# One load of w_phi, a split first tile, and later GpSimd readiness behind transfers in an attention and mixer kernel

## The chip, the cores and the metric

The kernel runs on one core of a Trainium2 chip. The metric is the time of one execution on the device in microseconds. Three runs of the kernel before took 1091.71, 1095.12 and 1089.41 us; the median is 1091.71.

## What is computed

The reference is a linear attention followed by a token and channel mixer, in float32. Shapes: 8 batches, 8 heads, 576 tokens, head dimension 64, 128 features, 512 channels, 256 hidden tokens, 1536 hidden channels.

```
phi(x)  = p = x @ w_phi;  p -= max|p| over features;  concat(exp(p), exp(-p))
kv      = phi(k)^T @ v              z = sum of phi(k) over tokens
x       = (phi(q) @ kv) / (phi(q) @ z + 1e-6)        # heads side by side: 512 channels
u       = x + w_tok2^T-side of relu(x^T @ w_tok1)    # mixes the 576 tokens
out     = u + relu(u @ w_ch1) @ w_ch2                # mixes the 512 channels
```

w_phi is 64x128. The mixer's weights come as float64.

## The kernel before

The work is recorded by five generators, and then ordered. `keys` and `queries` walk over 32 units; a unit is one batch and a pair of heads. Of the first eight units (PLAIN = 8) the tiles of q and k come together from `in_qkp`, q on partitions 0 to 63 and k on 64 to 127 (`load_plain`, L669: two tiles of 128x512 and 128x640, named `pair`). Later units come as `raw` and are split into a high and a low part on the partitions (`stack`, L609: a ScalarE cast and a GpSimd subtraction, into `stk` and `stq`).

`less_max` (L621) multiplies a tile with w_phi (`ppk`, `ppq`, `ppt` in PSUM, for keys, queries and the tail of a query), takes the largest absolute value (`mxk`, `mxq`, `mxt`) and subtracts it (`pmk`, `pmq`, `pmt`). In the first eight units this reads `wp`, a tile of 128x2x128. Its half 1 has w_phi on partitions 64 to 127 and zeros above, for the keys; its half 0 has w_phi on partitions 0 to 63 and zeros below, for the queries. Before the change w_phi is loaded twice, by two transfers on ScalarE's queue (L525 and L526), the keys' half first; GpSimd writes the zeros. Later two VectorE instructions for each half make `wp2` from it, which the later units use.

`turn` transposes pmq into `pt`, exponentiates it into `qf` and `qh`, and takes the low part `ql`, on VectorE for one sign and on GpSimd for the other. `numerators` (L854) multiplies with `kv` into `pn` and copies pn to `u0` and `u1`. The row of denominators then goes through a round of transfers on SP's queue: `few` (two small ones), a reciprocal, `inv` to DRAM, and two broadcasts of `inv` into parts of u0 and u1. At L883 GpSimd multiplies u0 and u1 into `xt`. Four such xt (two head pairs, two parts of the tokens) are the input of one half mix, `token_mix` (L897), which transposes xt into `px` on TensorE, and goes through `xh` and `xl`, `pa`, `ah` and `al` to `ph`; there are 16 such half mixes, two for a batch. The channel stream (`uh`, `ul`, `h`, `gh`, `gl`, `acc`) works on 18 blocks of 256 tokens and fills TensorE between the pieces of the others.

`weave` (L1039) interleaves the generators, and `arrange` (L276) makes one order from what was recorded: a greedy pass over a model of the five engines and one bus, with a planned start and end for each operation. An operation that waits for another gets a ready time from the end of that other and a lag (L470). On GpSimd and VectorE the next operation is the one with the earliest ready time, shifted by its stream. The end of a transfer is planned as its issue cost (560 ns for the broadcasts), its bytes at 210 per ns on the one bus, and 1400 ns, or 1000 for small ones (L43, L432). The instructions are then emitted sorted by planned start, so each engine works them off in that order. Since the pass is greedy, another ready time early on can change the order of everything behind it. The operations on `wp2` are emitted at 20 us of planned time.

Of the kernel before, what the change touches and what calls it, by code (L numbers as in the profile page):

```python
# [18 lines left out]
B, H, S, D = 8, 8, 576, 64  # L19
# [27 lines left out]
HOLD = 120.0  # L47
SLACK, EASE, CALM = 200, 1000, 8.0e5
PATIENCE = 0
LATER = 2.0e4  # L50
BEAT = 10240 / 3

# [202 lines left out]
def urge(op, t):  # L255
    if op.stream == "" or op.unit == "tensor":
        return op.pri
    return t + HEAD[op.stream]


def choose(ready, u, t, held):
    import heapq
    if u in ("vector", "gpsimd"):
        other = held["gpsimd" if u == "vector" else "vector"]
        if other > t + HOLD + PATIENCE:
            late = []
            while ready and (u == "gpsimd" or ready[0][2].shut):
                late.append(heapq.heappop(ready))
            got = heapq.heappop(ready) if ready else heapq.heappop(late)
            for x in late:  # L270
                heapq.heappush(ready, x)
            return got[2]
    return heapq.heappop(ready)[2]


def arrange(ops):  # L276
# [84 lines left out]
    def slots(r):  # L361
        if r.tag not in free:
            free[r.tag] = [0.0] * r.bufs
        return free[r.tag]

    def offer(op):
        r = op.first
        if r is not None:
            key = (r.tag, r.line)
            if turn[key] != r.place or not slots(r):  # L370
                waiting.setdefault(r.tag, []).append(op)
                return
            t = max(op.ready, min(slots(r)) + (LOAD if op.unit == "tensor" else 0.0))
        else:
            t = op.ready
        heapq.heappush(soon[op.unit], (t, op.pri, op.seq, op))
# [4 lines left out]
    def beat(end):  # L381
        while (beats[0] + 1) * BEAT <= end:
            share = spent.pop(beats[0], 0.0) / BEAT
            beats[0] += 1
            if slow[0]:
                slow[0] = share < 0.76
            else:
                slow[0] = share < 0.375

    def spend(t, end, work):  # L390
        k = int(t // BEAT)
        while k * BEAT < end:
            part = min(end, (k + 1) * BEAT) - max(t, k * BEAT)
            spent[k] = spent.get(k, 0.0) + work * part / (end - t)
            k += 1
    order, count = [], 0
    while count < len(ops):
        best = None
        for u in units:
            s, q = soon[u], ready[u]  # L400
            while s and s[0][0] <= clock[u]:
                t, pri, seq, op = heapq.heappop(s)
                heapq.heappush(q, (urge(op, t), seq, op))
            t = clock[u] if q else (s[0][0] if s else None)
            if t is not None and (best is None or t < best[0]):
                best = (t, u)
        if best is None:
            raise RuntimeError("nothing can be placed")
        t, u = best
        if ready[u]:  # L410
            op = choose(ready[u], u, t, held)
        else:
            op = heapq.heappop(soon[u])[3]
        r = op.first
        if r is not None:
            key = (r.tag, r.line)
            if turn[key] != r.place or not slots(r):
                waiting.setdefault(r.tag, []).append(op)
                continue
            have = slots(r)  # L420
            k = min(range(len(have)), key=lambda k: have[k])
            t = max(t, have.pop(k))
            turn[key] += 1
            again = waiting.pop(r.tag, [])
            for x in again:
                offer(x)
        op.start = t
        if op.name == "dma_start":
            t = max(t, BEGIN)
            clock[u] = t + op.cost  # L430
            bus[0] = max(t + op.cost, bus[0]) + op.bytes / RATE
            op.end = bus[0] + LANDING[0 if op.small else 1]  # L432
        elif u == "tensor":
            beat(t)
            pace = 2.0 if slow[0] else 1.0
            c = max(op.cost * pace if op.args[2].root.dtype != F32R or op.name == "transpose" else
                    max(op.cost, (op.cost - 4) * pace), LOAD * pace)
            rows = (op.args[1].lo, op.args[1].hi, op.args[0].lo, op.args[0].hi)
            if op.name == "transpose" or rows[1] - rows[0] == rows[3] - rows[2] == P:
                t = max([t, *(end + TURN for end in tiles.values())])  # L440
                tiles.clear()
                clock[u] = t + c
            else:
                t = max(t + (0 if tiles else TURN), tiles.get(rows, 0.0))
                tiles[rows] = t + c
                clock[u] = t + 14
            op.end = t + c + FILL
            spend(t, t + c, op.work * pace)
        else:
            op.end = t + op.cost  # L450
            if op.shut or u == "gpsimd":
                other = held["gpsimd" if u == "vector" else "vector"]
                op.end = max(op.end, other + op.cost - HOLD)
                held[u] = op.end
            clock[u] = op.end
        order.append(op)
        count += 1
        for r in op.roots:
            r.left -= 1
            r.done = max(r.done, op.end)  # L460
            if r.left == 0:
                slots(r).append(r.done + 40)
                for x in waiting.pop(r.tag, []):
                    offer(x)
        for x, soft in op.before:
            lag = 0.0 if x.unit == op.unit and u != "gpsimd" else LATE[x.unit]
            if soft or x.unit == op.unit == "tensor":
                got = op.start
            else:
                got = op.end + lag + (LOAD + (SLACK if op.end < CALM else EASE) if x.unit == "tensor" else 0.0)  # L470
            x.ready = max(x.ready, got)
            x.need -= 1
            if x.need == 0:
                offer(x)
    for op in order:
        if op.roots and op.roots[0].kw.get("name") == "wp2":
            op.start = LATER
    order.sort(key=lambda op: op.start)
# [4 lines left out]
def mixer_kernel(ctx, tc, qk, qkp, vals, w_phi, w1, w1t, w2, wc1, wc2d, out):  # L483
    real, nc = tc.nc, Recorder()
# [37 lines left out]
    make_identity(real, ident.made())  # L522
    wp2 = st.tile([P, 2, F], F32R, tag="wp2", name="wp2", bufs=1)
    wp = cst.tile([P, 2, F], F32, name="wp")
    for j in (1, 0):  # L525
        nc.scalar.dma_start(wp[j * D:j * D + D, j], w_phi)  # L526
    for j in (1, 0):
        nc.gpsimd.memset(wp[j * D:j * D + D, 1 - j], 0.0)
    ones = cst.tile([P, D], F32, name="ones")
# [139 lines left out]
    def load_plain(i):  # L669

        out = []
        for k, (c, n) in enumerate(((0, 512), (512, 640))):
            t = wk.tile([P, n], F32, tag=f"{'kq'[i % 2]}{k}", name=f"pair{i}{k}", bufs=1)
            nc.sync.dma_start(t, qkp[i, :, c:c + n])
            out.append(t)
        pairs[i] = out

    def keys():
# [3 lines left out]
        for i in range(B * NP):  # L682
            yield from until(lambda: i < 2 or i - 2 in asked)
            if i < PLAIN:
                load_plain(i)
            else:
                load(i)
# [378 lines left out]
    def never(mixed):  # L1066
        return False

    weave([(keys(), 5.2, bool), (queries(), 5.2, bool), (token_stream(), 8.0, lambda mixed: not mixed),
           (load_weights(), 10.0, never), (channel_stream(), 19.5, never)])  # L1070
    order = arrange(nc.ops)
    with tc.manual_schedule():
        for op in order:
# [52 lines left out]
```

## Time and profile before

| | |
|---|---|
| median of three runs | 1091.71 us |
| the profiled execution's own time | 1091.3 us |
| its span, first to last instruction | 1089.5 us |
| TensorE matmul busy | 1071.7 us, 98% |
| VectorE | 652.7 us, 60% |
| ScalarE | 585.3 us, 54% |
| GpSimd | 527.3 us, 48% |
| DMA | 65.24 MB, mean 60 GB/s |

In the profile PE is TensorE's matmul, PEld its weight load, DVE VectorE, ACT ScalarE, POOL GpSimd, SP the engine that issues most transfers; a q behind a name is the engine's queue of issues. Times of rows count from the span's start. A row names an instruction by what it writes and reads, out<-in; nearly all instructions have the line L175, a recorder's, so the tile names tell them apart. Idle time before an instruction stands in brackets, with what ended it.

### The profile page before, as it was taken

The page shows a single profiled execution, that of the slowest core. Times are in us where ns is not written, and L with a number is a line of the kernel's source. Part 1 is how long each engine was busy: PE and PEld are TensorE (multiplying, and loading weights), DVE is VectorE, ACT ScalarE, POOL GpSimd, SP SyncE. Part 2 cuts the span into 40 slices and gives each one's busy share as a digit, 9 for nine tenths or more (in the row PEclk, how much of TensorE's full clock was granted, in tenths as well). Part 3 has the DMA queues.
Part 4 walks back from the last instruction along what each step waited for, and adds up shares of the span by engine and source line. Part 5 has one row for each costly group of instructions (what it writes and reads, how often), then busy time and mean ns, then how long its engine had stood idle before and what let it go on. Part 6 is the DMA issues. An engine that isn't in the chain of part 4 may idle for free.

```text
span 1089.5 us, 23678 instructions
## 1 busy us (share of the span) xinstructions
PE 1071.7 (98%) x8880; PEld 1022.5 (94%) x8880; DVE 652.7 (60%) x1442; ACT 585.3 (54%) x1613; POOL 527.3 (48%) x660
## 2 busy tenths in 40 slices
PE   8999999999999999999999999999999999999998
PEld 7988997999999899999999999999999999999998
DVE  6898975566667667676666676676666543211111
ACT  5777654566656566566566566566666543211110
POOL 1244443566756565666556566575665633101110
PEclk9999999999999999999999999999999999999999
DMA  6565522111121211112121212112121101000000
GB/s 190 164 187 157 177 63 59 46 48 46 47 66 47 59 48 45 47 50 57 34 66 46 66 44 63 47 24 66 47 61 33 42 13 38 1 20 20 21 20 20
DMA packets 61090, 65.24 MB, mean 60 GB/s; under 512 B 28272, under 2 KB 47856, under 8 KB 60976
## 3 DMA queue, kind: packets, MB, share of 16 engines
q1 hardware_dynamic: 60672, 63.33, 21.0%
q8 instruction: 70, 1.15, 0.4%
q10 hardware_dynamic: 304, 0.40, 0.1%
q14 instruction: 44, 0.36, 0.1%
HBM read 53.97 MB, written 9.58 MB: 58 GB/s over the span
## 4 chain that ended last, share of the span: by engine, by line
PE 91%; DMA 3%; DVE 2%; issue 1%; POOL 1%; ACT 1%; SPq 0%; ACTq 0%; DVEq 0%; POOLq 0%
PE h L175 26%; PE acc L175 26%; PE pn L175 9%; PE pkv L175 8%; PE pa L175 5%; PE ph L175 4%; PE ppk L175 4%; PE ppq L175 3%; PE pt L175 3%; DMA u<-inv 2%; PE px L175 2%; DMA inv<-few 1%; PE pkt L175 1%; PE ppt L175 0%; POOL xt L175 0%
## 5 line engine op out<-in xcount | busy, mean ns | idle before, releaser
L175 PE MATMUL acc<-gh,wc 128*128 128x256 f32 x1728 | 332.5, 280 | 1.4 <-ACT gh L175 1.4
L175 PEld LDWEIGHTS acc<-gh,wc 128*128 128x128 f32 x1728 | 273.9, 188 | 2.9 <-ACT gh L175 1.8
L175 PE MATMUL h<-uh,wc_l 128*128 128x256 f32 x864 | 243.3, 282 | 0.0
L175 PE MATMUL h<-uh,wc_h 128*128 128x256 f32 x864 | 242.8, 281 | 0.2 <-DVE gl L175 0.2
L175 PE MATMUL acc<-gl,wc 128*128 128x256 f32 x864 | 242.6, 281 | 0.0
L175 PE MATMUL h<-ul,wc_h 128*128 128x256 f32 x864 | 242.1, 280 | 0.0
L175 DVE SCALAR_TENSOR_TENSOR gl<-h,gh 128x512 fp32r<-128x512 f32 x108 | 74.3, 688 | 158.1 <-ACT gh L175 157.3
L175 PEld LDWEIGHTS h<-uh,wc_h 128*128 128x128 f32 x864 | 162.7, 188 | 1.0 <-DVE gl L175 0.4
L175 PEld LDWEIGHTS h<-uh,wc_l 128*128 128x128 f32 x864 | 162.8, 188 | 0.9 <-issue 0.8
L175 PEld LDWEIGHTS h<-ul,wc_h 128*128 128x128 f32 x864 | 162.9, 189 | 0.4 <-issue 0.4
L175 PEld LDWEIGHTS acc<-gl,wc 128*128 128x128 f32 x864 | 162.9, 189 | 0.4 <-issue 0.4
L175 ACT ACTIVATE gh<-h 128x512 fp32r<-128x512 f32 x108 | 64.6, 598 | 155.9 <-PE h L175 154.6
L175 ACT ACTIVATE kp<-pmk 128x256 f32<-128x256 f32 (+1 forms) x320 | 110.9, 393 | 41.0 <-POOL pmk L175 16.4
L175 ACT ACTIVATE qf<-pt 128x256 f32<-128x256 f32 (+1 forms) x256 | 103.5, 416 | 54.5 <-PE pt L175 54.1
L175 POOL TENSOR_TENSOR ul<-xt,uh 128x64 fp32r<-128x64 f32 (+3 forms) x120 | 61.2, 540 | 125.8 <-ACT uh L175 125.3
L175 POOL TENSOR_TENSOR ql<-qf,qh 128x256 fp32r<-128x256 f32 (+1 forms) x96 | 81.1, 845 | 80.2 <-ACT qh L175 65.5
L175 POOL TENSOR_TENSOR pmk<-partk,mxk 128x256 f32<-128x256 f32 (+1 forms) x120 | 80.3, 672 | 58.0 <-DVE mxk L175 39.7
L175 POOL TENSOR_TENSOR xt<-u,u 128x256 f32<-128x256 f32 (+1 forms) x64 | 55.3, 865 | 97.9 <-DMA u<-inv 92.8
L175 PE MATMUL pn<-qh,kv 128*128 128x256 f32 (+1 forms) x384 | 94.3, 297 | 0.3 <-DVE xt L175 0.2
L175 DVE TENSOR_TENSOR ql<-qf,qh 128x256 fp32r<-128x256 f32 (+1 forms) x96 | 62.9, 655 | 47.9 <-ACT qh L175 47.8
L175 POOL TENSOR_TENSOR stq<-raw,stq 64x512 fp32r<-64x512 f32 (+1 forms) x48 | 72.0, 1500 | 34.8 <-ACT stq L175 24.4
L175 POOL TENSOR_TENSOR stk<-raw,stk 64x512 fp32r<-64x512 f32 (+1 forms) x48 | 68.4, 1439 | 30.6 <-ACT stk L175 28.9
(111 smaller groups left out, 2328.5 us busy)
## 6 DMA issues: line engine op xcount, KB each, us to landing
raw<-in_qk SPq DMA_DIRECT2D x23, 576.0 KB, 3.7
rawc<-in_wc SPq DMA_DIRECT2D x24, 512.0 KB, 4.5
v<-in_vals SPq DMA_DIRECT2D x31, 325.0 KB, 3.7
u<-inv SPq DMA_DIRECT2D x64, 80.0 KB, 3.2
u<-inv SPq DMA_DIRECT2D x64, 64.0 KB, 2.8
out_x<-xt SPq DMA_DIRECT2D x16, 192.0 KB, 2.0
out_x<-xt SPq DMA_DIRECT2D x11, 256.0 KB, 2.6
pair<-in_qkp SPq DMA_DIRECT2D x8, 320.0 KB, 3.9
```

Of the source, the lines that this page charges most:

```text
L175: return getattr(getattr(nc, self.unit), self.name)(*[real(a) for a in self.args], **{k: real(v) for k, v in self.kw.items()})
```

## The change

Three edits. w_phi is loaded once, into the keys' half, and VectorE copies it into the queries' half. The first tile of the first unit, 128x512, comes in two transfers of 256 columns. In the planner a GpSimd operation that depends on a transfer with a planned end past 260 us becomes ready 700 ns later than before; nothing else in the planner's model is touched.

```diff
--- before.py
+++ after.py
@@ -47,6 +47,7 @@
 HOLD = 120.0
 SLACK, EASE, CALM = 200, 1000, 8.0e5
 PATIENCE = 0
+STEADY, BEHIND = 2.6e5, 700.0
 LATER = 2.0e4
 BEAT = 10240 / 3
 
@@ -468,6 +469,8 @@
                 got = op.start
             else:
                 got = op.end + lag + (LOAD + (SLACK if op.end < CALM else EASE) if x.unit == "tensor" else 0.0)
+                if x.unit == "gpsimd" and op.name == "dma_start" and op.end > STEADY:
+                    got += BEHIND
             x.ready = max(x.ready, got)
             x.need -= 1
             if x.need == 0:
@@ -522,8 +525,8 @@
     make_identity(real, ident.made())
     wp2 = st.tile([P, 2, F], F32R, tag="wp2", name="wp2", bufs=1)
     wp = cst.tile([P, 2, F], F32, name="wp")
-    for j in (1, 0):
-        nc.scalar.dma_start(wp[j * D:j * D + D, j], w_phi)
+    nc.scalar.dma_start(wp[D:, 1], w_phi)
+    nc.vector.tensor_copy(wp[:D, 0], wp[D:, 1])
     for j in (1, 0):
         nc.gpsimd.memset(wp[j * D:j * D + D, 1 - j], 0.0)
     ones = cst.tile([P, D], F32, name="ones")
@@ -671,7 +674,9 @@
         out = []
         for k, (c, n) in enumerate(((0, 512), (512, 640))):
             t = wk.tile([P, n], F32, tag=f"{'kq'[i % 2]}{k}", name=f"pair{i}{k}", bufs=1)
-            nc.sync.dma_start(t, qkp[i, :, c:c + n])
+            for d in (0, n // 2) if i == k == 0 else (0,):
+                e = d + n // 2 if i == k == 0 else n
+                nc.sync.dma_start(t[:, d:e], qkp[i, :, c + d:c + e])
             out.append(t)
         pairs[i] = out
```

## Rows read from the trace of the kernel before

**Rows 1.** The page, busy time of TensorE: us, share of the span, instructions.

```profile
PE 1071.7 (98%) x8880; PEld 1022.5 (94%) x8880; DVE 652.7 (60%) x1442; ACT 585.3 (54%) x1613; POOL 527.3 (48%) x660
```

**Rows 2.** Busy time of each engine (x instructions), clock, DMA share, GB/s, by stretch.

```profile
0.00:260.00 260.00, 250.39 (x1934) 231.88 (x1935) 193.74 (x434) 164.49 (x434) 113.63 (x134) 1.00 0.41 118
260.00:950.00 690.00, 685.50 (x5751) 654.99 (x5750) 434.51 (x966) 401.17 (x1136) 401.85 (x505) 1.00 0.17 46
```

**Rows 3.** Timeline of the start: start us, us, engine, line, instruction, count, idle before.

```profile
0.74 1.20 ACTq L175 DMA_DIRECT2D wp<-in_w_phi  x2
...
0.75 1.93 SPq L175 DMA_DIRECT2D pair<-in_qkp  x4
...
3.76 0.93 PEld L175 LDWEIGHTS ppk<-wp,pair 128*128 128x128 f32 x4 [3.76 <-issue]
3.79 1.20 PE L175 MATMUL ppk<-wp,pair 128*128 128x128 f32 x4 [3.79 <-DMA wp<-in_w_phi]
...
5.65 1.22 PE L175 MATMUL ppq<-wp,pair 128*128 128x128 f32 x4 [0.67 <-DMA wp<-in_w_phi]
...
6.67 0.64 PE L175 MATMUL ppt<-wp,pair 128*128 128x128 f32 x2
...
6.91 0.42 DVE L175 TENSOR_REDUCE mxq<-ppq 128x2 f32<-128x256 f32 x1 [1.00 <-PE ppq L175]
```

**Rows 4.** Waits of TensorE from 260 us: us in total, times, longest us.

```profile
PE px L175 <- POOL xt L175: 2.5, 2, 1.4
PE pn L175 <- POOL ql L175: 1.5, 3, 1.1
```

**Rows 5.** DMA issues before 1.2 us: count, KB each, us to landing.

```profile
pair<-in_qkp SPq DMA_DIRECT2D x1, 320.0 KB, 3.2
pair<-in_qkp SPq DMA_DIRECT2D x1, 256.0 KB, 2.8
wp<-in_w_phi ACTq DMA_DIRECT2D x1, 32.0 KB, 3.0
```

**Rows 6.** Instructions on tile wp: count, ns minimum/median/maximum, first and last start.

```profile
L175 DVE CAST wp<-wp x2: 217/220/224, 19.5 to 20.1; 64x128 fp32r<-64x128 f32 x2
```

**Rows 7.** Groups of GpSimd from 260 us: busy us, mean ns, idle before, releasers.

```profile
L175 POOL TENSOR_TENSOR stk<-raw,stk 64x512 fp32r<-64x512 f32 (+1 forms) x40 | 57.1, 1443 | 27.9 <-ACT stk L175 26.6 <-POOL ql L175 0.5 <-POOL ul L175 0.2
...
L175 POOL TENSOR_TENSOR xt<-u,u 128x256 f32<-128x256 f32 (+1 forms) x46 | 39.5, 859 | 62.2 <-DMA u<-inv 57.1 <-DVE partk L175 3.5 <-PE h L175 0.5
```

**Rows 8.** DMA issues of u on the page: count, KB each, median us to landing.

```profile
u<-inv SPq DMA_DIRECT2D x64, 80.0 KB, 3.2
u<-inv SPq DMA_DIRECT2D x64, 64.0 KB, 2.8
```

**Rows 9.** Timeline of GpSimd near 350 us.

```profile
349.45 1.57 POOL L175 TENSOR_TENSOR stk<-raw,stk 64x640 fp32r<-64x640 f32 x1 [0.29 <-ACT stk L175]
353.71 0.74 POOL L175 TENSOR_TENSOR xt<-u,u 128x256 f32<-128x256 f32 x1 [2.69 <-DVE partk L175]
...
354.82 0.86 POOL L175 TENSOR_TENSOR ql<-qf,qh 128x320 fp32r<-128x320 f32 x1
```

**Rows 10.** Timeline of ScalarE near 350 us.

```profile
350.89 0.43 ACT L175 ACTIVATE qh<-pt 128x320 fp32r<-128x320 f32 x1
```

**Rows 11.** Timeline of TensorE at three waits past 260 us.

```profile
355.73 0.42 PE L175 MATMUL pn<-ql,kv 128*128 128x320 f32 x1 [1.08 <-POOL ql L175]
...
700.17 0.55 PE L175 MATMUL px<-ident,xt 128*128 128x128 f32 x3 [1.06 <-POOL xt L175]
...
878.59 0.55 PE L175 MATMUL px<-ident,xt 128*128 128x128 f32 x3 [1.45 <-POOL xt L175]
```

**Rows 12.** Timeline near 694 us, VectorE and GpSimd.

```profile
693.71 0.68 DVE L175 TENSOR_TENSOR ks<-kp,kp 128x512 f32<-128x512 f32 x1
...
694.22 1.32 POOL L175 TENSOR_TENSOR stq<-raw,stq 64x512 fp32r<-64x512 f32 x1 [0.87 <-ACT stq L175]
...
694.64 1.45 DVE L175 TENSOR_TENSOR ks<-ks,kp 128x512 f32<-128x512 f32 x1
```

## The prediction

> **What bounds the kernel now.** I read the page's engine line first: TensorE is busy for 1071.7 of 1089.5 us [rows 1]. Whatever the change does elsewhere, it can shorten the run only by what TensorE loses, so the next view is busy time by stretch [rows 2]. The granted clock is 1.00 in both stretches, so no part of the sum is a clock's. TensorE idles 260.00 - 250.39 = 9.6 us in the first 260 us and 690.00 - 685.50 = 4.5 us from there to 950; 3.7 us are left for the rest, channel work alone, which no edit touches. In the middle stretch GpSimd is busy 402 of 690 us and VectorE 435: both have slack, and what they cost is single late results.
>
> The 9.6 us of the beginning split into two parts. TensorE waits 3.79 us for the first w_phi transfer, runs the four ppk passes, and waits again, until 5.65, for the second, because ppq needs the other half of wp [rows 3]. The 9.6 - 3.8 - 0.7 = 5.1 us that are left are spread up to 260 us. In the middle stretch nearly every wait of TensorE names GpSimd: px waits 2.5 us for xt (2 times), pn 1.5 us for ql (3 times) [rows 4]. These 4.0 us are the largest sum that a better GpSimd order can return there. The run behind this trace took 1091.3 us, 1.8 more than its span; the median shown is 1091.71, 0.4 more. I sum from 1091.3 and add 0.4 at the end.
>
> **The change part by part.**
>
> *w_phi once.* The first load lands at 0.74 + 3.0 = 3.7 us [rows 3, 5]; the second lets ppq start at 5.65. The changed kernel has only the first, and a VectorE copy of 64x128 behind it. The trace has a cast of the same tile and shape at 0.22 us [rows 6]; with some 0.05 us of handover on each side (ppk's weight load starts 0.06 after the landing) the copy is done at 3.70 + 0.05 + 0.22 + 0.05 = 4.0 us. TensorE is then still in the four ppk passes: their weight loads end at 3.76 + 0.93 = 4.69 [rows 3]. So ppq starts at 4.69 and not at 5.65: 0.96 us less. The copy costs nothing beside that: behind it on VectorE stands mxk, which needs ppk's result and so the same load; without this cover the price would be its 0.22 us. ScalarE's queue loses one issue, 1.20 / 2 = 0.60 us [rows 3], so the v transfer and the table load behind it come that much earlier, which nothing waits for.
>
> Does the 0.96 us reach the end? VectorE is the engine nearest to a limit early on (194 of 260 us [rows 2]), but it stood idle 1.0 us before mxq for this very wait [rows 3], so its work moves forward too. What could eat it are the transfers behind, whose bytes are unchanged but for 32 KB. Bounds 0 and 1.0 us; I take 0.9.
>
> *First tile in two transfers.* The whole 256 KB tile lands at 0.75 + 2.8 = 3.55 us, w_phi at 3.7 [rows 5]: w_phi is the later of the two, so halving the tile saves nothing on the path. One more issue on SP costs the mean of the four pair issues, 1.93 / 4 = 0.48 us [rows 3], by which the later issues on SP slip. The next user is ppt, at 6.67 now and 5.7 after the change; its tile's issue is the second of the four and lands 3.2 us later, near 0.75 + 0.48 + 3.2 = 4.4 [rows 3, 5], at worst 4.9. I take 0; bounds 0.5 us gained (w_phi lands earlier because less runs beside it) and 0.5 us lost (a later tile is late by the slip).
>
> The Trainium skill, "DMA: Bandwidth & Descriptors", section "Anatomy of one DMA", gives 2.0 us plus bytes at 436 GB/s, measured on GpSimd's own path. By it w_phi would take 2.1 us and land at 2.8, half a tile at 3.05, and the first matmul would come some 0.6 us earlier: an estimate of 1087.7. The row says 3.0 us for w_phi, so I stay with the row.
>
> *GpSimd's order.* In the planner a GpSimd operation behind a transfer becomes ready 700 ns later, past 260 us of planned time. It is xt = u0*u1 that is moved by that: stq and stk also read a transfer, but they wait for ScalarE's cast of the same tile too, and 26.6 of stk's 27.9 us of waiting name ScalarE [rows 7]. 46 of the 64 xt run past 260 us of the trace [rows 7]; I treat plan and trace clocks as alike. For u, the code's landing estimate is 0.56 us of issue, 0.39 for 82 KB at its 210 bytes per ns, and 1.4: 2.35 us. The trace's median is 3.2, and 2.8 for the 64 KB ones, for which the code says 2.27 [rows 8]. So the plan is 0.5 to 0.85 us early on this step, and 700 ns is about that error.
>
> What it is worth I read off the waits. First, ql behind xt. At 351.02 GpSimd has finished stk and stands still for 2.69 us until xt at 353.71; ql comes after it at 354.82 [rows 9], though its input qh was done at 350.89 + 0.43 = 351.32 [rows 10], and pn waits 1.08 us for it [rows 11]. With xt placed later, ql goes into that gap and the 1.08 us are gone. The other two waits of this kind share 0.4 us, and I take nothing for them. Second, px on xt: at 700.17 (1.06 us) and 878.59 (1.45) TensorE had reached px before xt was there [rows 11]. Here GpSimd's order is not to blame, the transfer is; but the plan now believes in a later xt and puts up to 0.7 us of other matmuls ahead of px. That is 0.7 of each, 1.4 us. Together 2.5 us.
>
> Nothing on SP's queue waits for xt, and xt issues no transfer; what waits is the next writer of its u buffers, two pieces on. Bounds: 4.0 us gained if all waits of [rows 4] vanish; 4.0 us lost if the re-planned order, which changes as a whole because one greedy pass makes it, produces as many again. I take 2.5, nearest to the waits that I can follow one by one.
>
> The Trainium skill, "SBUF — State Buffer", section "Who interferes with whom", speaks against filling GpSimd's gaps: a VectorE instruction with two SBUF inputs and a GpSimd one that reads SBUF exclude each other. The trace agrees: ks takes 0.68 us at 693.71 and 1.45 at 694.64, beside stq [rows 12]. An estimate from that: if a quarter of the 46 xt [rows 7] sent a GpSimd instruction into such a meeting, at 0.77 us each, VectorE would lose 8.9 us of its 255 idle ones [rows 2]; were a quarter of it on TensorE's path the time would be 1090.5.
>
> Sum: 1091.3 - 0.9 - 2.5 = 1087.9, and 1088.3 on the footing of the median.
>
> **The rivals.**
>
> *Early waits go too (1085.5).* The 4.0 us of [rows 4] vanish and, with VectorE ahead by 1 us, half of the 5.1 us of early waits: 1091.7 - 0.9 - 4.0 - 2.5 = 1084.3; without the last term 1086.8; the middle is 1085.5. For it: the waits that the rows show one by one are at most 1.5 us, so a result that comes 0.7 us earlier ends much of them. Against it: the new order brings waits of its own.
>
> *It comes to nothing (1091.5).* The 0.9 us end in the next late transfer, and the new order swaps waits for others of the same size; or the copy is planned so late that ppq waits as before. For it: 4.5 us lost in 690 is little, and 57.1 of the 62.2 us that GpSimd idles before xt end with u's landing [rows 7], which no order makes earlier. Against it: the 1.08 us at 355.73 has a plain cause in the order.
>
> *xt late behind a busy GpSimd (1097.7).* If a ql, 0.86 us [rows 9], now stands before xt when u lands, xt and the px that waits for it come that much later. Each of the 16 half mixes needs four xt; 46 / 4 makes 12 of them past 260 us. In two of them px waits for xt today [rows 4]. It decides where TensorE reaches px less than 0.86 us after the landing. In 8 of 12 it costs 8 x 0.86 = 6.9 us: 1091.7 - 0.9 + 6.9 = 1097.7. Against it: the plan moves px by the same 700 ns, so TensorE meets it later.
>
> **How the numbers follow.** The forecast (1088.3, by itself 1086.3 to 1090.5) gets 0.46, early waits 0.21, nothing 0.25, late xt 0.08. A measurement here tells a change from none at about 0.5%, 5.5 us: faster is below 1086.2, slower above 1097.2. Faster takes most of the second case and the forecast's lower edge, 0.21; slower half of the last and a little of the third, 0.06; same 0.73. The range reaches from the second case's lower end, 1084.3, to 1094.8, where the GpSimd part costs its bound of 4.0 and the start still gives its 0.9.
>
> **What would show it.** Right: one w_phi issue, the copy near 3.75, ppq's first matmul near 4.7 directly behind ppk; in the middle stretch pn's wait for ql under 0.5 us and px's wait for xt at 1.1 or less, ql between stk and xt, TensorE's idle time from 260 to 950 at about 2 us. Wrong: ppq still near 5.6; a first matmul before 3.3 (then the half tile counted); TensorE's idle time in the first 260 us still at 9 us or more (the start was given back); px's wait on xt above 4 us.

## The result and the profile after

The changed kernel takes 1105.61 us (median of 4 runs, 1102.38 to 1107.41) against 1091.33 of the kernel before on the same chip: ratio 1.0125 [1.0109, 1.0141]. It is slower, 13.6 us by the ratio, where 3.4 us less was forecast. The chips of the later runs gave the kernel before 1091 to 1095.5 us, so kernels are compared by their ratio to it on the same chip. The profiled execution took 1107.4 us, its span 1105.6.

The page's engine line, against [rows 1]:

```profile
PE 1078.7 (98%) x8880; PEld 1026.9 (93%) x8880; DVE 655.1 (59%) x1443; ACT 585.0 (53%) x1613; POOL 531.9 (48%) x660
```

TensorE shows 7.0 us more busy time for the same 8880 matmuls. The stretches, in the columns of [rows 2], say how to read that:

```profile
0.00:260.00 260.00, 244.92 (x1855) 225.57 (x1856) 183.14 (x419) 159.23 (x419) 107.74 (x126) 0.99 0.41 116
260.00:950.00 690.00, 681.82 (x5695) 649.60 (x5694) 442.98 (x975) 402.90 (x1144) 411.58 (x511) 1.00 0.18 47
```

Idle time of TensorE rises from 9.6 to 15.1 us and from 4.5 to 8.2, together 9.2 of the 16.1 us of span. The counts tell the rest: 79 matmuls fewer are done by 260 us, another 56 fewer by 950. At 690.00 / 5751 = 0.12 us each that is 9.5 + 6.7 = 16.2 us, the whole difference of the spans. Not all of it is the change's. The trace before is an early one: in the nine later traces whose order departs from it only past 260 us of planned time, 1888 to 1928 matmuls are done by 260 us. Against the middle of the ten, 1906, the changed kernel lacks 51 by then, 6.1 us, and not 79. A matmul's end is modelled in the profile (0.28 us long, one every 0.115), so each interruption hides up to 0.16 us as busy time. Below, the lost work is read from the counts, with this spread in mind.

The start, in the columns of [rows 3]:

```profile
0.74 0.54 ACTq L176 DMA_DIRECT2D wp<-in_w_phi  x1
0.74 2.28 SPq L176 DMA_DIRECT2D pair<-in_qkp  x5
...
1.32 0.60 ACTq L176 DMA_DIRECT2D v<-in_vals  x1
...
3.17 0.22 DVE L176 COPY wp<-wp 64x128 f32<-64x128 f32 x1 [3.17 <-DMA wp<-in_w_phi]
...
3.24 1.19 PE L176 MATMUL ppk<-wp,pair 128*128 128x128 f32 x4 [3.24 <-DMA wp<-in_w_phi]
...
4.23 1.06 PE L176 MATMUL ppq<-wp,pair 128*128 128x128 f32 x4
...
5.08 1.06 PE L176 MATMUL ppk<-wp,pair 128*128 128x128 f32 x4
...
7.46 1.15 PE L176 MATMUL pkv<-v,kp 128*128 128x104 f32 x4 [1.32 <-DMA v<-in_vals]
...
8.41 0.67 PE L176 MATMUL ppt<-wp,pair 128*128 128x128 f32 x2
```

The first two steps came out better than forecast: first matmul at 3.24 instead of 3.79, ppq at 4.23 instead of 5.65, directly behind ppk. Then the order is another one: a ppk of the next keys and pkv stand ahead of ppt, and pkv waits 1.32 us for v. ppt runs at 8.41, 1.7 us later than before.

TensorE's waits past 260 us, in the columns of [rows 4]:

```profile
PE px L176 <- POOL xt L176: 2.5, 3, 1.1
PE px L176 <- DVE partq L176: 2.2, 2, 1.1
PE ppk L176 <- POOL stk L176: 1.6, 3, 0.7
```

pn's wait for ql has gone; px's for xt is as long as before, and waits for partq and stk are new. The largest single loss lies at 58 us. The timeline there:

```profile
51.07 1.19 SPq L176 DMA_DIRECT2D few<-u  x2
...
55.29 0.18 DVE L176 RECIPROCAL few<-few 128x4 f32<-128x4 f32 x1 [3.63 <-issue]
55.39 1.58 DVE L176 SCALAR_TENSOR_TENSOR bitsc<-rawc,bitsc 128x512 uint32<-128x512 uint32 x1
...
56.89 0.74 DVE L176 TENSOR_REDUCE mxq<-ppq 128x2 f32<-128x256 f32 x2
...
58.16 0.41 DVE L176 TENSOR_TENSOR pmq<-ppq,mxq 128x256 f32<-128x256 f32 x1
...
58.62 0.80 PE L176 MATMUL ppq<-wp,pair 128*128 128x128 f32 x2 [2.85 <-DVE pmq L176]
```

The reciprocal stands in VectorE's order where its `few` has only been asked for at 51.1 to 52.3; VectorE stands still for 3.63 us, then runs the bitsc that was planned next, and mxq and pmq, for which the next ppq waits, come last. The second of the two `few`, issued at 51.71, lands only 3.5 us later, at 55.2, just ahead of the reciprocal. TensorE waits 2.85 us. The busy time by stretch, columns as in [rows 2], shows a second price:

```profile
56.00:57.00 1.00, 0.00 (x0) 0.00 (x0) 1.00 (x2) 0.33 (x2) 0.42 (x1) 1.00 0.76 205
57.00:58.00 1.00, 0.00 (x0) 0.00 (x0) 1.00 (x3) 0.00 (x0) 0.00 (x0) 1.00 0.77 269
58.00:60.00 2.00, 1.38 (x7) 1.38 (x7) 0.90 (x3) 0.62 (x1) 1.04 (x1) 0.62 0.48 33
60.00:62.00 2.00, 2.00 (x11) 2.00 (x10) 0.43 (x2) 0.41 (x2) 0.23 (x1) 0.53 0.72 249
```

From 56 to 58 TensorE does nothing; behind that the granted clock is 0.62 and 0.53, most of the four microseconds at the 1.2 GHz level. At full clock they would have held (1 - 0.62) x 2 + (1 - 0.53) x 2 = 1.7 us more work.

### The profile page after: what moved, and what is told of

It reads as the page before. It is cut to its first block, busy times and chain, and to the rows that moved or that the text cites. A ratio compares the mean times of both kernels' runs of the same rounds, so it can differ in the third digit from the quotient of the medians.

```text
span 1105.6 us, 23696 instructions
## 1 busy us (share of the span) xinstructions
PE 1078.7 (98%) x8880; PEld 1026.9 (93%) x8880; DVE 655.1 (59%) x1443; ACT 585.0 (53%) x1613; POOL 531.9 (48%) x660
## 5 line engine op out<-in xcount | busy, mean ns | idle before, releaser
L176 POOL TENSOR_TENSOR ul<-xt,uh 128x192 fp32r<-128x192 f32 (+3 forms) x120 | 61.3, 545 | 114.5 <-ACT uh L176 114.3
L176 POOL TENSOR_TENSOR pmk<-partk,mxk 128x256 f32<-128x256 f32 (+1 forms) x120 | 81.9, 685 | 64.1 <-DVE mxk L176 51.1
L176 ACT ACTIVATE qh<-pt 128x256 fp32r<-128x256 f32 (+1 forms) x192 | 81.1, 422 | 0.0
```

The costliest lines, as they stand in the source:

```text
L176: return getattr(getattr(nc, self.unit), self.name)(*[real(a) for a in self.args], **{k: real(v) for k, v in self.kw.items()})
```

## The experiments

Each expectation names its theories for itself. Ratios are to the kernel before on the same chip, with their 95% intervals.

**Transfers and order, apart.** Four kernels split the change. The first keeps the order that was planned for the kernel before and only replaces the transfers when it is emitted:

```diff
         for op in order:
-            op.emit(real)
+            named = op.name == "dma_start" and isinstance(op.args[0], Part) and op.args[0].root.kw.get("name")
+            if named == "wp" and op.args[0].lo == 0:
+                real.vector.tensor_copy(wp[:D, 0].made(), wp[D:, 1].made())
+            elif named == "pair00":
+                for d in (0, 256):
+                    real.sync.dma_start(op.args[0][:, d:d + 256].made(), qkp[0, :, d:d + 256])
+            else:
+                op.emit(real)
```

> The order is planned as before; only when it is emitted does the second w_phi load become the VectorE copy and the first tile two transfers. TensorE and GpSimd keep the order of before to the last instruction. Theory A (the loss is the re-planned order, the new start itself is worth what its first 5 us show): about 1 us faster than before, 1089.5 to 1091, ppq near 4.2 us. Theory B (the new start costs by itself: one more SP issue, later landings behind it, VectorE's copy): 1098 or more, with the idle time of TensorE between 20 and 100 us near the changed kernel's 7 us. Theory C (GpSimd's 700 ns are to blame): as A here.

0.9991 [0.9974, 1.0009]. The copy and the two half tiles do what they did in the changed kernel, and no cost of theirs shows in the time. No gain shows either. Timeline and DMA issues (count, KB each, us to landing):

```profile
0.75 0.86 SPq L1079 DMA_DIRECT2D pair<-in_qkp  x2
1.33 0.60 ACTq L175 DMA_DIRECT2D v<-in_vals  x1
1.65 1.37 SPq L175 DMA_DIRECT2D pair<-in_qkp  x3
...
4.21 1.06 PE L175 MATMUL ppq<-wp,pair 128*128 128x128 f32 x4
...
7.77 0.79 PE L175 MATMUL ppt<-wp,pair 128*128 128x128 f32 x2 [2.49 <-DMA pair<-in_qkp]
```

```profile
v<-in_vals ACTq DMA_DIRECT2D x1, 325.0 KB, 6.2
pair<-in_qkp SPq DMA_DIRECT2D x1, 320.0 KB, 6.1
```

ppt waits 2.49 us for the second tile, which lands at 1.65 + 6.1 = 7.7. Its issue is now the third on SP, and the 325 KB of v, on ScalarE's queue, are issued 0.3 us ahead of it; they land at 1.33 + 6.2 = 7.5. The 1.4 us won at ppq end here.

The second is the opposite: the changed kernel's order with the old transfers (the copy left out, the second w_phi load and the whole tile put back when it is emitted).

> The reverse: planned as in the changed kernel, but the two loads of w_phi and the whole first tile are emitted, so the work of before runs in the changed order. Theory A: as slow as the changed kernel or a little slower, 1104 to 1108, with the stall of TensorE near 56 us and the slow clock behind it. Theory B: the 9 us that the first 260 us lost come back, 1096 to 1099.

1.0152 [1.0129, 1.0175]: the loss is in the order. The stall is there too (VectorE stands still for 3.79 us, TensorE for 3.07), but no slow clock follows it: from 54 to 68 us the granted clock is 1.00 throughout. The third and fourth re-plan, each with one half of the change: `BEHIND` alone, and the start alone (the diff's w_phi and tile parts).

> Only the 700 ns of GpSimd past 260 us of planned time; the order of all engines is that of before up to there (TensorE's first 1312 rows). Theory A (two re-plannings, of which the early one costs 9 us and the later one 7): the first 260 us as before, and either 1098 if the 7 us lost behind them belong to the 700 ns, or 1088 to 1094 if they belong to the order that the new start left. Theory C: 1100 or more. The forecast's own step, 2.5 us gained: 1088.8.

> w_phi once and the split tile, planned anew, without the 700 ns: the order differs from the third matmul group on. Theory A: about 1100.5 if the later 7 us belong to the 700 ns, 1104 to 1108 if any new order loses them; the stall near 56 us is there in both. Theory C: 1090 to 1092.

`BEHIND` alone costs 1.0086 [1.0061, 1.0111], the start alone 1.0043 [1.0027, 1.0058]; the sum is the whole loss, within the intervals. So both halves have their price: the 700 ns alone are in theory C's range, and the start costs half of the early loss that theory A took from the counts (1100.5 is a ratio of 1.0084). In the start alone VectorE stands still 3.40 us ahead of the same reciprocal, ppq waits 2.2 us for pmq, and the granted clock is 0.66 from 60 to 65 us, so the stall at 58 us belongs to this half. In `BEHIND` alone the middle stretch and its waits are those of the changed kernel:

```profile
260.00:950.00 690.00, 681.58 (x5685) 648.50 (x5685) 443.14 (x967) 400.82 (x1134) 405.78 (x505) 1.00 0.19 47
```

66 matmuls fewer than [rows 2], 7.9 us. Near 404 us its timeline shows one of the two waits for partq:

```profile
403.64 2.15 DVE L176 TENSOR_TENSOR ks<-ks,kp 64x256 f32<-64x256 f32 x2
...
403.95 1.56 POOL L176 TENSOR_TENSOR stq<-raw,stq 64x640 fp32r<-64x640 f32 x1 [1.25 <-issue]
...
406.17 0.41 DVE L176 TENSOR_TENSOR partq<-ppq,partq 128x256 f32<-128x256 f32 x1
...
406.64 0.41 PE L176 MATMUL px<-ident,xt 128*64 128x128 f32 x2 [1.15 <-DVE partq L176]
```

The two ks instructions take 2.15 us together, where the shortest ks of this trace takes 0.39; they end at 405.8, just behind stq, which ends at 405.5. partq and px come that much later. At 645.91 the same four rows stand once more.

**Which transfer is late.** Three kernels in the order of the kernel before: the copy of w_phi alone, the split alone, and both with v of the first unit issued on SP's queue behind the second tile.

```diff
...
+            else:
+                if named == "v0":
+                    op.unit = "sync"
+                op.emit(real)
```

> The order of before, with only the second w_phi load emitted as the VectorE copy; the first tile whole. Theory D (the second tile of unit 0, 320 KB, landed at 7.7 us and not at 4.4 because v's transfer moved ahead of it when one ScalarE issue went): the second tile lands at 6 us or later, ppt waits 1 us or more for it. Theory E (the split's extra SP issue pushed it back): the second tile lands near 4.4, ppq starts near 4.7, ppt behind it near 5.7, and the first pn comes about 1 us earlier than before's 17.5. In time both lie within 0.2% of before.

> The order of before, with only the first tile in two transfers; w_phi loaded twice. Theory D: the second tile lands at 5 us or earlier, ppq still waits for the second w_phi load until 5.6. Theory E: the second tile lands at 6 us or later and ppt waits for it. In time both lie within 0.2% of before.

> The order of before and the whole new start, but v of unit 0 is issued on SP behind the second tile, no longer on ScalarE. Theory D: the second tile lands near 4.4, ppt follows ppq at about 5.1 to 5.7 without a wait, and the first pn comes 1 to 1.5 us earlier than 17.5 unless v, now later (near 8.5), holds pkv; 0.1% faster than before. Theory E: the second tile lands at 6 us or later all the same.

0.9990 [0.9976, 1.0004], 0.9994 [0.9982, 1.0007] and 0.9977 [0.9960, 0.9994]. With the copy alone ppq starts at 4.77, and ppt at 5.62 without a wait: v is issued as early as 1.33, but the second tile before it. The expectation that this tile would be late already here was wrong. With the split alone the tile is issued at 1.65 and v at 1.96, and the tile's issue row is

```profile
pair<-in_qkp SPq DMA_DIRECT2D x1, 320.0 KB, 4.6
```

It lands at 6.25, where the prediction had 4.4. Theory D was wrong here too: the split by itself makes the tile late. Nobody waits for it, because ppq gets its second w_phi load only at 5.26, and ppt follows ppq at 6.29. The copy takes that cover away and moves v ahead of the tile, which lands 1.5 us later still, at 7.7. With v behind the tile:

```profile
1.66 0.42 SPq L175 DMA_DIRECT2D pair<-in_qkp  x1
2.13 0.43 SPq L175 DMA_DIRECT2D v<-in_vals  x1
...
4.30 1.06 PE L175 MATMUL ppq<-wp,pair 128*128 128x128 f32 x4
...
5.54 0.80 PE L175 MATMUL ppt<-wp,pair 128*128 128x128 f32 x2 [0.18 <-DMA pair<-in_qkp]
```

The tile lands at 5.5, and the time is 0.23% [0.06, 0.40] below before, though the intervals of the four kernels with the order of before overlap. The expected 17.5 for the first pn was an early execution's: in the ten traces that begin as the kernel before does, ppq starts at 5.06 to 6.87 and the first pn runs at 17.46 to 19.14. With v behind the tile it runs at 17.41, with the copy alone at 17.22: earlier than in all ten, whose middle is 18.4, so about a microsecond of the start's gain is there.

Re-planned with v on SP's queue (`nc.sync` for all of v's loads, and the two start edits), without `BEHIND`:

> w_phi once and the split tile, planned anew, with v of unit 0 issued on SP behind the second tile, so that plan and chip both have it there; no 700 ns. TensorE's order differs from before in 327 rows, that of the same edits with v on ScalarE in 715. Theory J (the 0.4% that the new start lost were v and the second tile changing places, in the chip's transfers and in the plan): 0.997 to 1.000, no wait of TensorE over 1 us between 5 and 100 us. Theory K (any order that the plan makes of the new start loses early): 1.003 or more, with the stall near 56 us and the slow clock behind it.

0.9999 [0.9986, 1.0012]. The 0.43% are back, the stall at 58 us is gone, and the first 100 us have other waits instead: px 2.9 us for xt, in two, the longer of 1.6 us. From 55 to 60 us the granted clock is 0.66. So theory J's time came true, and its "no wait over 1 us" did not.

**What the 700 ns do.** First the collision of ks and stq near 404 us. The second half of ks is emitted behind partq or partk where it stood one or two places ahead of it; `BEHIND` stays at 700. The expectation counts 11 such places; VectorE's order in the two traces differs in 8.

> The kernel with the 700 ns alone, but where the second ks half (two SBUF inputs) stood just ahead of a partq or partk on VectorE, it is emitted behind it (11 places). Theory F (part of the loss is that GpSimd's moved stq holds VectorE's ks, and partq behind it then holds px's PSUM bank): px's 2.3 us of waits for partq are gone, and the time falls by about 2 us, from 1.0086 of before to 1.007. Theory G (the waits come from the order as a whole and this one is replaced by another): the time stays within 0.1%, with new waits of px of the same sum.

1.0066 [1.0049, 1.0084]: what theory F forecast, and not to be told from `BEHIND` alone either. The waits for partq are gone, so the ks ahead of it was their cause; but ppk now waits 3.1 us for stk, and 5683 matmuls are done in the middle stretch instead of 5685. Whether some 2 us came back stays open; most of the loss did not.

Then GpSimd's order alone: where another of its instructions follows an xt at once in the plan, xt goes behind it, in 34 places of the trace, and all other engines keep their order.

> The order of before on all engines but one: past 260 us of planned time an xt that the plan follows at once by another GpSimd operation is emitted behind that one (33 GpSimd instructions change place; TensorE, VectorE, ScalarE and SP keep their order). This is the forecast's step by itself. The forecast: pn's waits for ql (1.5 us) go, px's waits for xt stay near 2.5 us or grow by up to 0.8 us each; 0 to 1.5 us faster than before. Theory I (a later xt is itself the harm): 3 us slower or more, with px's waits for xt at 5 us or more. Theory H (the harm is the re-planned order of TensorE and the others): 0.999 to 1.001 of before.

1.0003 [0.9993, 1.0013]. TensorE's waits:

```profile
PE px L175 <- POOL xt L175: 2.9, 3, 1.6
PE pn L175 <- POOL ql L175: 0.4, 2, 0.3
```

ql waits fall from 1.5 to 0.4 us, px's for xt go from 2.5 to 2.9. In the five traces in which all engines keep the order of before past 260 us, the first are 1.1 to 1.7 and the second 0.8 to 3.5: the 0.4 is the edit's, the 2.9 says nothing. So the direct effect of the reordering is about 1 us of ql's waits, which the time does not show.

Then re-planning as such: 5 ns more for a VectorE operation behind a ScalarE one past 260 us, by itself and on top of the 700; and other values of `BEHIND`.

```diff
+                if x.unit == "vector" and op.unit == "scalar" and op.end > STEADY:
+                    got += 5.0
```

> Before, with 5 ns instead of 700, and on other instructions: a VectorE operation that waits for ScalarE becomes ready 5 ns later past 260 us of planned time. GpSimd's readiness is untouched; but TensorE's order differs in as many places (3762 rows) as with the 700 ns (3728). Theory H: slower than before by several us, 1.004 to 1.010, with new waits of TensorE of the same kinds. Theory I: 0.998 to 1.002.

> 700 ns for GpSimd as in the change, and the 5 ns for VectorE behind ScalarE that alone moved nothing in time. TensorE's order differs from that of the 700 ns alone in 2669 rows, from row 1723 on. Theory I2: 1.007 to 1.010, the 700 ns cost the same in another order. Theory H2: 0.999 to 1.004, nearer to the nudge alone; px's waits for partq (2.3 us) and ppk's for stk (1.3 us) are gone.

> The GpSimd edit alone with 350 ns. TensorE's order differs from row 2050 on (2896 rows). Theory I: about half of the 8 to 9 us that 700 ns cost, 1.003 to 1.005. Theory H: no relation to the size; anything from 1.000 to 1.010, later start of the differences notwithstanding.

> The GpSimd edit alone with 850 ns. TensorE's order differs from that of 700 ns in 2901 rows and from that of 1000 in 3155. If the loss falls with the size between 700 and 1000: 1.003 to 1.006. If 700 is one bad spot (all values from 690 to 750 give nearly the same order): 0.998 to 1.002.

> The GpSimd edit alone with 1000 ns, between the 700 that cost 0.9% and the 1400 that gained 0.16%. Theory I2 (the size decides: up to some size the new waits outweigh the old, above it px's and pn's waits go): 1.002 to 1.006, in between. Theory H2 (what decides is the single order that a value happens to give; most orders lie within 0.2% of before, the one of 700 does not): 0.998 to 1.002.

> The GpSimd edit alone with 1400 ns, twice the change's. Theory I: 1.013 or more. Theory H: no relation to the size, 1.000 to 1.010.

| | ratio | matmuls, 260 to 950 us | idle, us |
|---|---|---|---|
| before | 1 | 5751 | 4.5 |
| 5 ns, no BEHIND | 1.0001 [0.9990, 1.0012] | 5730 | 5.3 |
| BEHIND 350 | 1.0014 [0.9999, 1.0029] | 5723 | 6.6 |
| BEHIND 700 | 1.0086 [1.0061, 1.0111] | 5685 | 8.4 |
| BEHIND 700 and 5 ns | 1.0079 [1.0058, 1.0100] | 5707 | 6.1 |
| BEHIND 850 | 1.0008 [0.9998, 1.0018] | 5744 | 5.0 |
| BEHIND 1000 | 1.0000 [0.9986, 1.0014] | 5760 | 2.8 |
| BEHIND 1400 | 0.9984 [0.9971, 0.9997] | 5755 | 3.0 |

The table takes the middle stretch because the early one also differs from execution to execution: `BEHIND` 350 keeps TensorE's old order for its first 2458 matmuls and yet had done 1905 by 260 us, not 1934. The middle one is not free of that: with v behind the tile, in the order of before, TensorE did

```profile
260.00:950.00 690.00, 683.12 (x5714) 651.89 (x5713) 436.12 (x966) 400.12 (x1130) 400.43 (x502) 1.00 0.19 46
```

and was no slower. Only the 5685 lies well below that. The 5 ns change TensorE's order in as many rows as the 700 (3762 and 3728) and cost nothing that can be measured, so theory H, by which any new order loses, is out. The theories of size fail at 350, 850, 1000 and 1400. 700 costs 0.8 to 0.9% in two different orders, while 850 costs 0.2% at most. In the second of the two the waits for partq and stk are gone and others stand there (h 1.5 us for gl). At 1000 the middle stretch is what the forecast expected of 700, and yet the time is that of the kernel before:

```profile
260.00:950.00 690.00, 687.20 (x5760) 656.42 (x5759) 436.78 (x967) 402.20 (x1136) 404.02 (x506) 1.00 0.18 46
```

**The change with 1000, and a better version.** The changed kernel with `BEHIND = 1000.0`; and an order planned as before with 1400, emitted with the new start and v of the first unit on SP.

> The changed kernel with 1000 ns in place of 700. If the change's 1.25% are 0.4% of its start and 0.9% of what 700 ns does, this comes to 1.003 to 1.006 of before, TensorE's idle time from 260 to 950 us falls from 8 to 3 or 4 us, and the early stall near 56 us stays. If the start and the 700 ns make each other worse, it stays above 1.008.

> What the runs point to: the order planned as before with 1400 ns for GpSimd, the new start put in when it is emitted, v of unit 0 on SP behind the second tile. If the two gains add: 0.9977 x 0.9984 = 0.996 of before; px's waits for xt and pn's for ql past 260 us gone, ppt behind ppq without a wait over 0.3 us.

With 1000 the change costs 1.0038 [1.0024, 1.0053]: the loss of `BEHIND` is gone, and what is left is as large as the start's (1.0043 by itself). But the traced execution, the fastest of its six, does not have the early stall that was expected to stay: the second `few` lands 1.8 us after its issue, the reciprocal waits 1.60 us, and the granted clock from 50 to 70 us is 1.00. The mean granted clock of the other five is 0.998, as in seven of eight executions of the start alone, so they may have the stall and the slow clock; that is not shown. The best version has 0.9970 [0.9954, 0.9986], 1091.57 us against 1094.78, faster than before and than the change. From the 0.9977 of the new start with v behind the tile it can't be told, so it is not shown that the two gains add. Its middle stretch:

```profile
260.00:950.00 690.00, 687.35 (x5754) 656.75 (x5754) 437.04 (x967) 402.66 (x1139) 404.45 (x510) 1.00 0.18 47
```

## Why the prediction was wrong

*The copy of w_phi: right.* The copy takes 0.22 us beside ppk and ppq follows ppk without a gap, at 4.23, or 4.77 with the copy alone (4.69 forecast). How much of the 0.9 us reaches the end is not shown: 0.9990 [0.9976, 1.0004] fits all of it and none.

*The split at 0: too low.* The step took w_phi as the later transfer, which the split cannot help. w_phi lands 2.4 or 2.5 us after its issue with the split, 3.0 in [rows 5] without: the first matmul runs at 3.20 to 3.31 in the eight traces with the split, at 3.78 with the copy alone. For the first matmul the bound of 0.5 us gained was the right value; but the split's bound on the loss, a second tile late by 0.5 us at most, was too small, as the next step shows. The Trainium skill, "DMA: Bandwidth & Descriptors", section "Anatomy of one DMA", whose fit gave the first matmul 0.6 us earlier, agrees with these rows in the result, 0.55; its 2.1 us for w_phi does not (2.4 here, 3.0 in [rows 5]).

*"the v transfer and the table load behind it come that much earlier, which nothing waits for": failed.* The prediction asked who waits for v, and not what v would run beside. With its issue at 1.33 it came ahead of the second tile, whose issue the split had moved to 1.65. Not "near 4.4, at worst 4.9" but 6.25 was the tile's landing with the split alone, where the wait for w_phi hid it, and 7.7 with both edits in the old order, where ppt waited 2.49 us for it. Two edits, each without a cost in the time by itself, met in transfers that the text had counted for each alone.

*The order early on: failed.* No term stood for re-planning the first 260 us; the start's worst case was 0.5 us lost, by the split. Re-planned with the new start alone, the kernel loses 0.43%, 4.7 us, of which the stall near 58 us (2.85 us and 1.7 of clock in the changed kernel) is the largest shown part. The greedy pass put the reciprocal ahead of work that was ready, in a plan that lands a small transfer 1000 ns after its issue and its bytes, where this `few` took 3.5 us; why the new start leads it there was not traced further.

*GpSimd's order: mechanism half right, the bound on its price failed.* ql's waits went as the step said, px's for xt did not. The step asked which of today's waits would go, and bounded the new ones by the sum of the old, 4.0 us. The re-planned order lost 0.86%, 9.4 us; the counts of one trace put 7.9 of it in the middle stretch, though two traces of the old order differ by up to 42 matmuls, 5 us, there. The bound had no reason behind it: a new order can bring waits of other kinds, at other places, than the old one had. The rule that the prediction weighed and priced at 2.2 us, the Trainium skill, "SBUF — State Buffer", section "Who interferes with whom", is at work in it: the two ks beside stq, 2.15 us, and their wait are that exclusion. It explains 2.3 us of waits at most, not 9.4. VectorE's added busy time is no measure of the loss: it is 8.6 us in `BEHIND` alone and 11.2 in the 5 ns kernel, which loses nothing.

What makes 700 bad and 850 not is open. Two orders share the loss and not the waits that the profile names, and with one of these waits removed most of the loss stayed.

*The rivals.* None of the three was it. Late xt came nearest in sign, but px's waits for xt did not grow. For the two direct effects, each put into the old order, the second rival was near: 0.9991 and 1.0003.

## What to carry to other kernels

Where one greedy pass plans everything, an edit has two prices: the thing itself, and the new order. Emit the edit in the old order and the new order without the edit, and the two come apart in two runs; a tuned constant should be tried at its neighbours before it is believed or blamed. A wait of one trace should be set against several traces of one order first: here px's wait for xt was 0.8 to 3.5 us with nothing in the order changed. When an edit shortens one queue and lengthens another, list the issues of both in the order of time: a large transfer that was second may now be first.

## What the runs showed of the hardware

A 320 KB transfer on one queue landed 6.1 us after its issue when 325 KB had been issued on another queue 0.3 us earlier, and 4.6 us when they were issued there 0.3 us later: 1.5 us for the place in time. With the 325 KB behind it on its own queue it took 3.8. A transfer of 1 KB landed 1.8 us after its issue in one execution and 3.5 in another, at the same place of the order. And about 2 us without a matmul were followed in the changed kernel by some four at the lower of TensorE's two clocks, so a wait of 2.85 us cost about 4.5. But the kernel with the old transfers in the new order stood 3.07 us at the same place, and no microsecond behind it was at the lower clock.
